# Attention and two gated layers in one kernel: the order in which the next pair's q and k are prepared, the padding of the last keys' v, and the place of three weight conversions

## The chip, the cores and the metric

The kernel runs on one core of a Trainium2 chip. The metric is the device time of one execution in microseconds (us), as the median of the runs shown. Profile numbers come from one further execution that was recorded instruction by instruction.

## The reference

The reference is a thresholded attention followed by two gated layers. There are 4 batches of 8 heads, 576 positions and 64 dimensions a head; q, k and v are float32, the weights float64.

```
scores = scale * q @ k.T                       # per head, 576 x 576
thresh = max(scores, -1) - tau
scores = where(scores >= thresh, scores, -1e9)
attn   = exp(scores - max) / (sum + 1e-9)
x = (attn @ v) as 2304 tokens x 512
g = x @ w_gate;  x = (silu(g) * (x @ w_val)) @ w_out         # 512 -> 1536 -> 512
h = (x @ w1) * (x @ w2) @ w3;  out = h @ w_out2              # 512 -> 1024 -> 512
```

## The kernel before

Each float32 operand of a matmul is split into a high part of TensorE's short float type and the low remainder, and products are summed from both parts. Splitting is therefore everywhere: a high part is a rounding copy, a low part a subtraction.

**Attention** goes over 16 pairs of heads (p, four pairs to a batch). One pair has nine tiles (i = 0 to 8): four row blocks of 128 for each head, and tile 4, which holds the last 64 rows of both. For each tile `mm_scores` makes scores in one of two S banks of PSUM, `el_max` (L482, VectorE) takes the negative row maximum and moves the scores to P, `el_exp` (L491, ScalarE) makes the exponential, and `el_mask` (L501, VectorE) applies the threshold. Scores are issued two tiles ahead, masks two tiles behind, so that the scores of the next pair's first tile are issued in tile 7 of this one.

The **main queue** holds the work behind the masks: transposes of P through TensorE (`it_T`, `it_kl`, `it_lq`, `it_corner`), each split on its way out of PSUM on one of three paths (`evac_split`), and the products with v (`it_pv`). Five items of a pair are queued behind its tile 4's mask, eleven behind tile 8's, which is two tiles into the next pair. The **prep queue** holds the preparation of the next pair. `it_k` and `it_q` transpose k and q through TensorE and copy the high part out on ScalarE (khi, qhi); `it_k2` and `it_q2` subtract it in PSUM by a matmul (`less`), copy out the low part (klo, qlo), and stack high and low parts into the operands L and R by twelve DMAs on SyncE's queue (`stack`, L348 and L349). `it_left` transposes the last 64 rows of q and k (L421) and writes LZ and part of R (L313). Every transpose, split and product with v takes one of four T banks of PSUM. `some` gives both queues credit: 19.5 main items for nine tiles, 0.8 prep items a tile. What is appended to `deferred` by one item runs after the next one (`run_item`). The compiler orders each engine's instructions by a simulated time with the program's order as priority; so instructions can move ahead of their place in the program where buffers allow it.

**The last keys' v.** 64 rows of v behind the first 512 are split for a whole batch by `split_left` into vls; `split_v` copies each pair's share by two DMAs into VLZ, which holds zeros in the other head's half of the partitions.

**Weights** come as float64 and are turned into float32 in place of two halves. `conv_step` loads raw words (three buffers, 512 KB each, L128), takes them apart on VectorE (L139, L142, L145) and ScalarE (L148, L149) and joins them on GpSimd (L150); one step later `conv_value` finishes (L157) and `conv_unit` splits the value into a slot of two parts (L196, L199, the latter in turn on GpSimd and VectorE). The **slots** are shared by weights and token blocks: 3 from the start (u1), 7 more at the last pair's start (u2), 8 more near its end (u3), 24 after attention (u4). In the last pair `early` interleaves three conversion steps with the preparation of x block 0 (`x_prep`, four pieces; each takes two raw slots for its loads, L790 and L795, adds on GpSimd at L826, multiplies on VectorE at L829 and splits at L817 and L818). The gated layer's matmuls (L835) on x block 0 need all four pieces and the first three weight units.

Of the kernel before, what the change touches and what calls it, by code (L numbers as in the profile page):

```python
# [23 lines left out]
N_U1, N_U2, N_U3, N_U4 = 3, 7, 8, 24  # L24
N_TMP, N_BIG, N_HB, N_TA = 6, 3, 3, 1

GROUP = 2

# [6 lines left out]
def kernel(  # L35
# [171 lines left out]

    def conv_step(n=1):

        old = []  # L210
        while conv_mid and conv_mid[0][2]() and len(old) < n:
            old.append(conv_mid.popleft())
            old[-1][1](conv_value(old[-1][0]))
# [14 lines left out]
    def attention(actx, early, tail):  # L228
# [8 lines left out]
        ta = lctx.enter_context(tc.tile_pool(name="ta", bufs=N_TA))  # L237
        raw_i, in_tail = [0], []

        def raw_tile():  # L240
            raw_i[0] += 1
            if in_tail or raw_i[0] % (N_TA + N_TMP) >= N_TA:
                return tmp()
            return ta.tile([P, 512], F32, tag="raw", name="raw")

# [7 lines left out]
        VLZ = at.tile([P, 2, 2, 2, D], F32R, name="VLZ")  # L253
        nc.gpsimd.memset(f32(VLZ), 0.0)

# [29 lines left out]
        def split_left(b):  # L285
# [11 lines left out]
            vls = wk.tile([P, HP, 2, D], F32R, tag="vls", name="vls", bufs=2)  # L297
            split_pool(vls[:, :, 0, :], vls[:, :, 1, :], vl)
            lsplit[b] = (qks, vls)

        def split_v(p):
# [4 lines left out]
            vls = lsplit[p // HP][1]  # L306
            for h in range(2):
                r = slice(64 * h, 64 * h + 64)
                nc.sync.dma_start(out=f32(VLZ[r, p % 2, h]), in_=f32(vls[r, p % HP]))
            load(p + 2, (2,))  # L310

# [39 lines left out]
        halves = {}  # L351

        def it_q(p):
            hi = sp.tile([P, 512], F32R, tag="qhi", name="qhi")
            halves[p, 0] = (turn(raws.pop((p, 0)), hi, 0.125), hi)

        def it_k(p):
            hi = sp.tile([P, 512], F32R, tag="khi", name="khi")
# [774 lines left out]
```

## Time and profile before

| | |
|---|---|
| median of 3 runs | 1189.6 us (1189.56 to 1189.74) |
| profiled execution | 1189.26 us |
| its span, first to last instruction | 1187.3 us |
| TensorE matmul busy | 1122.1 us, 95% |
| TensorE weight load busy | 959.8 us, 81% |
| VectorE busy | 733.1 us, 62% |
| ScalarE busy | 590.3 us, 50% |
| GpSimd busy | 475.7 us, 40% |
| mean granted TensorE clock | 0.991 of full speed |

PE is TensorE, PEld its weight loads (they overlap the matmuls), DVE VectorE, ACT ScalarE, POOL GpSimd, SP SyncE. Busy time is the union of an engine's instructions in a stretch. A matmul's end is modelled, so that a PE that is busy throughout need not be at its peak rate. L12 is line 12 of the kernel; where a helper issues an instruction, the line is the helper's. "t_bank<-ident,P" names what an instruction writes and reads.

### The profile page before, as it was taken

The page shows a single profiled execution, that of the slowest core. Times are in us where ns is not written, and L with a number is a line of the kernel's source. Part 1 is how long each engine was busy: PE and PEld are TensorE (multiplying, and loading weights), DVE is VectorE, ACT ScalarE, POOL GpSimd, SP SyncE. Part 2 cuts the span into 40 slices and gives each one's busy share as a digit, 9 for nine tenths or more (in the row PEclk, how much of TensorE's full clock was granted, in tenths as well). Part 3 has the DMA queues.
Part 4 walks back from the last instruction along what each step waited for, and adds up shares of the span by engine and source line. Part 5 has one row for each costly group of instructions (what it writes and reads, how often), then busy time and mean ns, then how long its engine had stood idle before and what let it go on. Part 6 is the DMA issues. An engine that isn't in the chain of part 4 may idle for free.

```text
span 1187.3 us, 16882 instructions
## 1 busy us (share of the span) xinstructions
PE 1122.1 (95%) x6074; PEld 959.8 (81%) x6074; DVE 733.1 (62%) x1272; ACT 590.3 (50%) x1071; POOL 475.7 (40%) x457
## 2 busy tenths in 40 slices
PE   7898998899878999999999999999899999999998
PEld 6788888788766777888888888888787888888886
DVE  7987868778798797656464664567892022432222
ACT  6877878778786456443242432345563231321111
POOL 4575665565663655443232332234241221321110
PEclk9999999999989999999999999999999999999999
DMA  8865756656455743222111120123430010100024
GB/s 197 224 146 141 163 132 142 146 121 142 107 170 167 216 126 100 75 68 71 31 59 36 37 89 8 47 93 103 124 107 18 1 36 1 37 1 1 1 58 102
DMA packets 107891, 108.14 MB, mean 91 GB/s; under 512 B 48800, under 2 KB 82208, under 8 KB 107808
## 3 DMA queue, kind: packets, MB, share of 16 engines
q1 hardware_dynamic: 107808, 107.06, 34.3%
q8 instruction: 48, 0.79, 0.3%
q14 instruction: 35, 0.29, 0.1%
HBM read 68.16 MB, written 14.23 MB: 69 GB/s over the span
## 4 chain that ended last, share of the span: by engine, by line
PE 55%; DVE 5%; DMA 2%; ACT 1%; issue 1%; POOL 0%; POOLq 0%; DVEq 0%; ACTq 0%
PE t_bank L835 36%; PE s_bank L835 19%; DMA raw<-in_moe_w_dram 2%; DVE tmp L157 1%; DVE slot L818 1%; DVE raw L142 1%; DVE tmp L145 1%; DVE tmp L139 0%; DVE slot L911 0%; PE t_bank L908 0%; DVE slot L199 0%; DVE slot L1022 0%; DVE slot L882 0%; DVE slot L1059 0%; ACT raw L148 0%
## 5 line engine op out<-in xcount | busy, mean ns | idle before, releaser
L835 PE MATMUL t_bank<-slot,slot 128*128 128x512 f32 (+1 forms) x2592 | 559.7, 371 | 5.9 <-DVE slot L818 2.4
L835 PEld LDWEIGHTS t_bank<-slot,slot 128*128 128x128 f32 x2592 | 457.0, 189 | 92.8 <-DVE slot L818 3.3
L835 PE MATMUL s_bank<-h,slot 128*128 128x512 f32 (+1 forms) x720 | 161.9, 372 | 3.4 <-ACT slot L884 2.2
L150 POOL TENSOR_TENSOR raw<-raw 128x512 int32<-128x512 int32 x76 | 84.4, 1111 | 182.1 <-ACT raw L149 171.6
L501 DVE SCALAR_TENSOR_TENSOR P<-P,stat,E 128x576 f32<-128x576 f32 x144 | 148.3, 1043 | 5.6 <-POOL stat L474 3.9
L835 PEld LDWEIGHTS s_bank<-h,slot 128*128 128x128 f32 x720 | 126.8, 190 | 27.1 <-ACT slot L884 2.6
L482 DVE TENSOR_SCALAR_CACHE_REDUCE P<-s_bank,neg 128x576 f32<-128x576 f32 x144 | 114.2, 809 | 55.2 <-PE s_bank L443 55.2
L1069 DVE TENSOR_TENSOR tmp<-tmp,t_bank 128x512 f32<-128x512 f32 (+1 forms) x40 | 25.3, 633 | 178.2 <-PE t_bank L835 178.2
L107 POOL TENSOR_TENSOR h<-tmp,h 128x512 fp32r<-128x512 f32 (+1 forms) x60 | 74.4, 1239 | 136.1 <-ACT h L106 136.0
L1073 POOL TENSOR_TENSOR h<-tmp,h 128x512 fp32r<-128x512 f32 (+1 forms) x38 | 45.8, 1205 | 200.5 <-ACT h L1071 200.5
L491 ACT ACTIVATE E<-P,stat 128x576 f32<-128x576 f32 x144 | 116.4, 812 | 9.7 <-DVE P L482 8.8
L443 PE MATMUL s_bank<-R,L 128*128 128x288 f32 x512 | 101.2, 318 | 14.7 <-DVE P L482 5.6
L920 DVE TENSOR_TENSOR tmp<-tmp,t_bank 128x512 f32<-128x512 f32 (+1 forms) x60 | 37.9, 631 | 113.1 <-PE t_bank L835 104.5
L835 PE MATMUL s_bank<-slot,h 128*128 128x512 f32 x432 | 106.6, 391 | 0.9 <-DVE slot L1059 0.8
L328 PE MATMUL t_bank<-ident,P 128*128 128x128 f32 x640 | 90.5, 277 | 14.5 <-DVE AT L524 4.7
L443 PEld LDWEIGHTS s_bank<-R,L 128*128 128x128 f32 x512 | 76.8, 194 | 26.7 <-DVE P L482 15.1
L835 PEld LDWEIGHTS s_bank<-slot,h 128*128 128x128 f32 x432 | 79.9, 188 | 18.3 <-DVE slot L1059 2.1
L882 DVE TENSOR_TENSOR slot<-s_bank,slot 128x1024 f32<-128x1024 f32 (+1 forms) x72 | 82.2, 1146 | 18.5 <-PE s_bank L835 16.5
L328 PEld LDWEIGHTS t_bank<-ident,P 128*128 128x128 f32 x640 | 74.2, 141 | 23.5 <-DVE ATL L524 4.6
L583 PE MATMUL t_bank<-AT,sp 128*128 128x288 f32 x512 | 87.5, 307 | 5.3 <-DVE AT L524 2.4
L157 DVE SCALAR_TENSOR_TENSOR tmp<-tmp,raw 128x512 f32<-128x512 f32 x76 | 72.0, 948 | 30.5 <-POOL raw L150 30.5
L919 ACT ACTIVATE tmp<-t_bank 128x512 f32<-128x512 f32 (+1 forms) x60 | 33.2, 554 | 113.3 <-PE t_bank L835 106.9
(110 smaller groups left out, 1427.9 us busy)
## 6 DMA issues: line engine op xcount, KB each, us to landing
raw<-in_moe_w_dram SPq DMA_DIRECT2D x32, 512.0 KB, 3.8
raw<-in_moe_w_out_dram SPq DMA_DIRECT2D x20, 512.0 KB, 3.5
x_dram<-xs SPq DMA_DIRECT2D x64, 144.0 KB, 2.4
L<-qhi SPq DMA_DIRECT2D x60, 128.0 KB, 2.9
L<-qlo SPq DMA_DIRECT2D x60, 128.0 KB, 2.5
raw<-in_moe_w_gate_dram SPq DMA_DIRECT2D x12, 512.0 KB, 3.7
raw<-in_moe_w_val_dram SPq DMA_DIRECT2D x12, 512.0 KB, 3.8
ld<-in_k_dram SPq DMA_DIRECT2D x16, 256.0 KB, 4.0
```

What stands on the lines that cost most here:

```text
L107: nc.gpsimd.tensor_tensor(out=lo, in0=src, in1=f32(hi), op=ALU.subtract)
L150: nc.gpsimd.tensor_tensor(out=a, in0=a, in1=x, op=ALU.subtract)
L157: nc.vector.scalar_tensor_tensor(out=f32(m), in0=f32(m), scalar=2.0 ** 20, in1=f32(a), op0=ALU.add, op1=ALU.mult)
L328: nc.tensor.matmul(bank[:, t * P:(t + 1) * P], lhsT=part, rhs=ident, is_transpose=True, start=(t == 0), stop=(t == len(parts) - 1),)
L443: nc.tensor.matmul(o, lhsT=lhs, rhs=R[:, c:c + HALF], start=(h == hs2[0] and e == 0), stop=(h == hs2[-1] and e == 1),)
L482: nc.vector.tensor_scalar(out=p_tile(p, i).rearrange("p (a c) -> p a c", a=2), in0=sb[:, :, 0:HALF], scalar1=neg, scalar2=None, op0=ALU.mu ...
L491: nc.scalar.activation(out=e, in_=p_tile(p, i), func=ACTF.Exp, scale=-1.0, bias=stats[p // HP][:, 0, c:c + 1],)
L501: nc.vector.scalar_tensor_tensor(out=t, in0=t, scalar=stats[b][:, 1, c:c + 1], in1=e, op0=ALU.is_le, op1=ALU.mult, accum_out=sums[b][:, c: ...
L583: nc.tensor.matmul(o, lhsT=vs[:, 4 * h + c, :, :].rearrange("p a d -> p (a d)"), rhs=AT[h][:, e, c, cs], start=(c == 0 and e == 0), stop=F ...
L835: nc.tensor.matmul(o, lhsT=lhs(a), rhs=rhs(c), start=(first and i == 0), stop=(last and i == 2))
L882: nc.vector.tensor_tensor(out=a, in0=s, in1=a, op=ALU.add)
L1073: (nc.vector if end else nc.gpsimd).tensor_tensor(out=h[:, 1, 0:n], in0=ab[:, 0:n], in1=f32(h[:, 0, 0:n]), op=ALU.subtract)
```

## The change

Three things change. First, `turn` takes both halves of the split: it transposes, copies the high part out, and appends the second half with its stacking DMAs to `deferred`; `it_k2` and `it_q2` are gone as items, and the prep queue is given 1.0 items a tile. Second, `split_left` writes the last keys' v straight into zero-padded tiles, one for each of two batches, by four GpSimd instructions on 64 partitions each; vls and the two DMAs a pair are gone. Third, in tile 4 of pairs 3, 6 and 9 a conversion step and its finishing half (`conv_end`) are added to the prep queue, so that the first three weight units fill the slots of u1 there; `early` keeps x block 0 alone, the raw loads at half of attention are gone, u2 has one slot less and u3 one more, and the extra buffer for raw evacuations (`ta`) is gone.

```diff
-N_U1, N_U2, N_U3, N_U4 = 3, 7, 8, 24
-N_TMP, N_BIG, N_HB, N_TA = 6, 3, 3, 1
+N_U1, N_U2, N_U3, N_U4 = 3, 6, 9, 24
+N_TMP, N_BIG, N_HB = 6, 3, 3
+EARLY = (3, 6, 9)
...
+    def conv_end(n=1):
+        old = 0
+        while conv_mid and conv_mid[0][2]() and old < n:
+            bits, done, _ = conv_mid.popleft()
+            done(conv_value(bits))
+            old += 1
+        return old
...
     def conv_step(n=1):
-        old = []
-        while conv_mid and conv_mid[0][2]() and len(old) < n:
-            old.append(conv_mid.popleft())
-            old[-1][1](conv_value(old[-1][0]))
+        old = conv_end(n)
...
-        VLZ = at.tile([P, 2, 2, 2, D], F32R, name="VLZ")
-        nc.gpsimd.memset(f32(VLZ), 0.0)
+        VLZ = [at.tile([P, HP, 2, 2, D], F32R, name=f"VLZ{n}") for n in range(2)]
+        for t in VLZ:
+            nc.gpsimd.memset(f32(t), 0.0)
...
-            vls = wk.tile([P, HP, 2, D], F32R, tag="vls", name="vls", bufs=2)
-            split_pool(vls[:, :, 0, :], vls[:, :, 1, :], vl)
-            lsplit[b] = (qks, vls)
+            for h in range(2):
+                r = slice(64 * h, 64 * h + 64)
+                split_pool(VLZ[b % 2][r, :, h, 0, :], VLZ[b % 2][r, :, h, 1, :], vl[r])
+            lsplit[b] = qks
...
-            vls = lsplit[p // HP][1]
-            for h in range(2):
-                r = slice(64 * h, 64 * h + 64)
-                nc.sync.dma_start(out=f32(VLZ[r, p % 2, h]), in_=f32(vls[r, p % HP]))
...
-        def turn(raw, hi, scale):
+        def turn(raw, hi, lo, scale, then):
             bank = t_bank()
             turn_p(bank, [raw[:, t, :, :].rearrange("p h d -> p (h d)") for t in range(4)])
             nc.scalar.activation(out=hi, in_=bank, func=ACTF.Copy, scale=scale)
-            return bank
-        def turn_lo(bank, hi, lo, scale):
-            less(bank, minus_r if scale == 1.0 else minus8_r, hi)
-            nc.scalar.activation(out=lo, in_=bank, func=ACTF.Copy, scale=scale)
+            def rest():
+                less(bank, minus_r if scale == 1.0 else minus8_r, hi)
+                nc.scalar.activation(out=lo, in_=bank, func=ACTF.Copy, scale=scale)
+                then()
+            deferred.append(rest)
...
-                raw = raw_tile()
+                raw = tmp()
...
-            return [lambda f=f: f(p) for f in (it_k, it_q, it_k2, it_q2, it_left)]
+            return [lambda f=f: f(p) for f in (it_k, it_q, it_left)]
...
-            credit[1] += (1.5 if in_tail else 0.8) * frac
+            credit[1] += (1.5 if in_tail else 1.0) * frac
...
-            if n == NS // 2:
-                conv_fetch()
+            if i == 4 and p in EARLY:
+                prep.extend([conv_step, conv_end])
...
-        r = [conv_step] * 3
-        for kk in range(KD):
-            r.insert(2 * kk + 1, lambda kk=kk: x_prep(0, kk))
-        return r
+        conv_fetch()
+        return x_items(0)
```

## Rows read from the trace of the kernel before

**Rows 1.** The page, part 1: busy us, share of the span, instructions.

```profile
PE 1122.1 (95%) x6074; PEld 959.8 (81%) x6074; DVE 733.1 (62%) x1272; ACT 590.3 (50%) x1071; POOL 475.7 (40%) x457
```

**Rows 2.** Stretches: bounds, us, busy us of each engine, PEclk, DMA share, GB/s.

```profile
core 0: us, PE busy (x) PEld busy (x) DVE busy (x) ACT busy (x) POOL busy (x), PEclk, DMA share, GB/s
176.78:191.17 14.39, 11.88 (x87) 10.60 (x85) 13.58 (x34) 13.78 (x27) 9.90 (x11) 1.00 0.70 163
191.17:198.06 6.89, 6.89 (x55) 6.82 (x56) 2.64 (x7) 3.70 (x12) 1.69 (x2) 1.00 0.44 101
...
47.62:329.77 282.15, 254.29 (x1827) 231.79 (x1828) 226.72 (x517) 228.85 (x463) 169.36 (x191) 0.99 0.61 142
329.77:361.00 31.23, 22.90 (x136) 19.51 (x135) 31.23 (x58) 25.36 (x47) 18.94 (x16) 0.89 0.58 170
...
456.00:814.00 358.00, 358.00 (x1752) 303.45 (x1753) 205.59 (x279) 135.59 (x218) 123.03 (x104) 1.00 0.19 60
```

**Rows 3.** Waits, 16 to 330 us: who waited for whom, us, times, longest.

```profile
DVE P L482 <- PE s_bank L443: 50.6, 16, 6.3
```

**Rows 4.** Timeline of ACT in pair 8: start us, us, line, operation.

```profile
179.54 0.62 ACT L340 ACTIVATE khi<-t_bank 128x512 fp32r<-128x512 f32 x1
...
182.41 0.66 ACT L345 ACTIVATE klo<-t_bank 128x512 fp32r<-128x512 f32 x1
...
184.26 0.60 ACT L340 ACTIVATE qhi<-t_bank 128x512 fp32r<-128x512 f32 x1 [0.45 <-PE t_bank L328]
...
186.65 0.61 ACT L345 ACTIVATE qlo<-t_bank 128x512 fp32r<-128x512 f32 x1
...
194.99 0.39 ACT L313 ACTIVATE R<-t_bank 128x128 fp32r<-128x128 f32 x2
```

**Rows 5.** Timeline of SyncE's queue in pair 8.

```profile
180.19 0.49 SPq L348 DMA_DIRECT2D R<-khi  x1
...
184.25 0.66 SPq L282 DMA_DIRECT2D ld<-in_q_dram  x1
...
190.83 0.60 SPq L349 DMA_DIRECT2D L<-qhi  x1
```

**Rows 6.** Timeline of PE at the end of pair 8.

```profile
186.02 0.70 PE L443 MATMUL s_bank<-R,L 128*128 128x288 f32 x4
...
191.12 0.51 PE L443 MATMUL s_bank<-R,L 128*128 128x288 f32 x2 [0.85 <-DVE P L501]
...
194.22 0.46 PE L421 MATMUL t_bank<-ident_r,qkls 128*128 128x128 f32 x4
```

**Rows 7.** Timeline of DVE at the end of pair 8.

```profile
196.88 0.82 DVE L482 TENSOR_SCALAR_CACHE_REDUCE P<-s_bank,neg 128x576 f32<-128x576 f32 x1 [4.25 <-PE s_bank L443]
```

**Rows 8.** Groups on DVE, 330.5 to 358.4 us: count | busy us, mean ns | idle.

```profile
L157 DVE SCALAR_TENSOR_TENSOR tmp<-tmp,raw 128x512 f32<-128x512 f32 x3 | 4.2, 1411 | 0.0
...
L145 DVE SCALAR_TENSOR_TENSOR tmp<-raw,tmp 128x512 f32<-128x512 uint16 x3 | 2.4, 816 | 0.0
L142 DVE TENSOR_SCALAR raw<-raw 128x512 int32<-128x512 int32 x3 | 2.4, 812 | 0.0
...
L199 DVE TENSOR_TENSOR slot<-tmp,slot 128x512 fp32r<-128x512 f32 x1 | 1.7, 1749 | 0.0
L139 DVE TENSOR_SCALAR tmp<-raw 128x512 int32<-128x512 int32 x3 | 1.2, 455 | 0.0
```

**Rows 9.** Groups on ACT in the same stretch.

```profile
L148 ACT ACTIVATE raw<-raw,ebias 128x512 int32<-128x512 int32 x3 | 2.3, 758 | 1.0 <-DVE tmp L145 1.0
```

**Rows 10.** Timeline of SyncE's queue in pair 1.

```profile
38.61 0.60 SPq L128 DMA_DIRECT2D raw<-in_moe_w_gate_dram  x1
```

**Rows 11.** Timelines of the last pair: SyncE's queue, and all engines.

```profile
326.43 0.55 SPq L790 DMA_DIRECT2D slot<-x_dram  x1
...
360.66 0.68 DVE L818 TENSOR_TENSOR slot<-tmp,slot 128x512 fp32r<-128x512 f32 x1
```

**Rows 12.** VLZ's instructions (min/median/max ns), and groups of the first 650 us.

```profile
L309 SPq DMA_DIRECT2D VLZ<-vls x32: 461/476/1601, 10.2 to 329.6; - x32
...
L103 POOL TENSOR_TENSOR vls<-vl,vls 128x256 fp32r<-128x256 f32 x4 | 3.6, 894 | 0.2
```

More of the change, by code (lines that the diff above doesn't have):

```diff
@@ L236, in attention @@
         sp = lctx.enter_context(tc.tile_pool(name="sp", bufs=1))
[L237 to L244, printed above, removed]
+        in_tail = []
         ATT = at.tile([P, 2, 2, 4, S], F32R, name="AT")
@@ L305, in split_v @@
             splits[p, 2] = t
-            vls = lsplit[p // HP][1]
-            for h in range(2):
-                r = slice(64 * h, 64 * h + 64)
-                nc.sync.dma_start(out=f32(VLZ[r, p % 2, h]), in_=f32(vls[r, p % HP]))
             load(p + 2, (2,))
+        deferred = deque()
         def scaled(out_, in_, scale=1.0):
@@ L349, in stack, with then @@
             nc.sync.dma_start(out=f32(dst[64:P, :]), in_=f32(bottom[64 * h:64 * h + 64, :]))
-        halves = {}
         def it_q(p):
+            L, R = qk_tiles(p)
             hi = sp.tile([P, 512], F32R, tag="qhi", name="qhi")
-            halves[p, 0] = (turn(raws.pop((p, 0)), hi, 0.125), hi)
+            lo = sp.tile([P, 512], F32R, tag="qlo", name="qlo")
+            def then():
+                stack(L[:, 0, :], lo, hi, 0)
+                stack(L[:, 1, :], hi, lo, 1)
+                stack(L[:, 2, :], hi, lo, 0)
+                stack(L[:, 3, :], lo, hi, 1)
+            turn(raws.pop((p, 0)), hi, lo, 0.125, then)
         def it_k(p):
+            L, R = qk_tiles(p)
             hi = sp.tile([P, 512], F32R, tag="khi", name="khi")
-            halves[p, 1] = (turn(raws.pop((p, 1)), hi, 1.0), hi)
-        def it_q2(p):
-            L, R = qk_tiles(p)
-            bank, hi = halves.pop((p, 0))
-            lo = sp.tile([P, 512], F32R, tag="qlo", name="qlo")
-            turn_lo(bank, hi, lo, 0.125)
-            stack(L[:, 0, :], lo, hi, 0)
-            stack(L[:, 1, :], hi, lo, 1)
-            stack(L[:, 2, :], hi, lo, 0)
-            stack(L[:, 3, :], lo, hi, 1)
-        def it_k2(p):
-            L, R = qk_tiles(p)
-            bank, hi = halves.pop((p, 1))
             lo = sp.tile([P, 512], F32R, tag="klo", name="klo")
-            turn_lo(bank, hi, lo, 1.0)
-            stack(R[:, 0:512], hi, lo, 0)
-            stack(R[:, 640:1152], lo, hi, 1)
+            def then():
+                stack(R[:, 0:512], hi, lo, 0)
+                stack(R[:, 640:1152], lo, hi, 1)
+            turn(raws.pop((p, 1)), hi, lo, 1.0, then)
         def turn_r(parts, dst):
@@ L412, in it_left @@
             L, R = qk_tiles(p)
-            qks = lsplit[b][0]
+            qks = lsplit[b]
             bank = t_bank()
@@ L504, in el_mask @@
             )
-        deferred = deque()
         path_i = [0]
@@ L588, in it_pv @@
                 nc.tensor.matmul(
-                    o, lhsT=VLZ[:, p % 2, h, :, :].rearrange("p a d -> p (a d)"),
+                    o, lhsT=VLZ[b % 2][:, hp, h, :, :].rearrange("p a d -> p (a d)"),
                     rhs=ATL[:, e, cs], start=False, stop=(e == 1),
```

## The prediction

> **What bounds the kernel now.** The page comes first. TensorE (PE) is busy 95% of the span [rows 1], so I looked for the stretches where it is not. The view of stretches gives three regimes. From 456 to 814 us PE is busy 358.0 of 358.0 us: nothing that moves work on another engine helps there, and whatever is saved earlier shifts this block forward whole. From 329.8 to 361.0, the last pair of heads (pair 15), VectorE (DVE) is busy 31.23 of 31.23 us and PE 22.90. In the thirteen steady pairs 2 to 14, from 47.62 to 329.77 us, no engine is full: PE 254.3, DVE 226.7, ScalarE (ACT) 228.9 of 282.15 us [rows 2]. That is 21.7 us a pair, with 17.6 us of ACT work in it.
>
> Cutting one steady pair in two shows why. Pair 8 begins with its first exponential at 176.78 and runs its nine tiles until 191.17; ACT is busy 13.78 of these 14.39 us and DVE 13.58. Then come 6.89 us until pair 9's first exponential, in which PE is busy throughout, but ACT only 3.70 us and DVE 2.64 [rows 2]. The two halves hardly overlap. In the table of waits for 16 to 330 us, DVE's row-maximum instruction waits 50.6 us for score matmuls, in only 16 waits of 3.2 us each, about one for each pair boundary [rows 3].
>
> What those scores wait for is seen by following the preparation of pair 9 through pair 8, times from pair 8's start. The first half of k leaves ACT at +2.8 us (khi), its second at +5.6 (klo), the first half of q at +7.5 (qhi), its second at +9.9 (qlo) [rows 4]. Twelve stacking DMAs follow on SyncE's queue, one each 0.6 us when it isn't waiting; the first goes at +3.4, the last is issued at +14.1 [rows 5]. Pair 8's last scores run at 186.02; the first two matmuls of pair 9 start 4.4 us behind them, at 191.12 (+14.3), with the last stacks. The left-over rows' transposes (`it_left`) come at 194.22 (+17.4) [rows 6], write R at 194.99 [rows 4], and the first maximum of pair 9, which needs that column of R, starts at 196.88 [rows 7]. The other boundaries have the same order: stacks, first scores, `it_left`, maximum. So the period is set by a chain of preparation whose last two links, q's second half and `it_left`, are late because they stand late in the program.
>
> **The change, part by part.**
>
> *Order of the preparation.* Before, five items at 0.8 a tile: credit reaches 1, 2, 3, 4, 5 in tiles 1, 2, 3, 4 to 5 and 6, so `it_left` is emitted in tile 6, behind nearly all of the previous pair's transposes and P·V items, whose PSUM banks it then follows. After, three items at 1.0 a tile: `it_k` in tile 0, `it_q` in tile 1, `it_left` in tile 2; k's second half runs behind `it_q`, q's behind the next main item. No instruction of k, q or the left-over rows is added or removed. `it_q` and `it_left` now stand ahead of the P·V items. With khi still at about +2.8, q's transposes come one item behind k's, qlo some 3 us earlier, and the stacks run nearly back to back: 12 of 0.6 us plus the two loads of the pair after next (0.7 us each) from +3.4 end near +12 rather than +14.1. `it_left` is done by about +8. Then the first scores may start near +12, the maximum 1.5 us later and the exponential 1.2 us after that (196.88 to 198.06 here): a chain of about 15 us instead of 21.7. It no longer decides; what is late next is engine work: ACT's 17.6 us a pair, and PE's 19.6 busy. So a pair may fall to anything between 17.6 and 21.7 us. Four in-order queues with all this work interleaved will not fill any of them: I take 20.6, a little over a quarter of the way down. 13 pairs x 1.1 us = **-14.3 us**. Bounds: 0 and -36 (18.9 us a pair, ACT at 93%).
>
> *Three units of weights in pairs 3, 6 and 9.* Each costs, in the last pair's rows, DVE 4.0 us (L139, L142, L145, L157 and every second time L199: 1.2 + 2.4 + 2.4 + 4.2 + 1.7 = 11.9 for three) [rows 8], and ACT two conversions of 0.76 us (L148, and L149 like it) [rows 9] and a cast of 128x512, 0.62 as khi's [rows 4], 2.1 us in all; GpSimd takes the rest. They now fall into tiles 5 and 6 of a pair, where ACT and DVE are nearly full. ACT is 81% busy over the pairs, so I charge 0.81 x 2.1 = 1.7 us each, **+5.1 us**. Bounds: 0 (in the idle part) and 4.0 each, 12. The first three raw loads were already issued at 38.6 us although the program has them at pair 8 [rows 10]; the compiler's order pulls loads ahead, so I cost their move at nothing. Three more raw loads of 512 KB move to pairs 3, 6 and 9 behind the freeing of a raw buffer; they stand on SyncE's queue in front of P·V outputs, not of stacks, which are done by tile 5: nothing, or 1 us each if they hold up a stack.
>
> *The last pair.* The 11.9 us of DVE work above leave a stretch in which DVE is full for 31.23 us [rows 2, 8]. Cover is not the question, but what is late next: the first GLU step needs all four pieces of x block 0. Their first load goes at 326.43, and the last one's low half is written by 361.34 [rows 11]: 8.7 us a piece, with DVE full. After, 6 free slots stand where 10 stood; four become x block 0, so one pair of raw slots serves the four pieces in turn: load, GpSimd add, DVE multiply, next load. The trace has no such chain; with DVE free I estimate 7.5 us a piece, 30 in all (bounds: 4 us, if loads and arithmetic overlap, and 11), and it may start earlier, since the stacks and `it_left` of pair 15, whose buffers lie in its place, end earlier. Saved: at most 11.9, I take **-8 us**; at worst 0. Behind 361 the count of conversions ahead of the GLU steps is the same from the second step on, so the gain should be carried through to the block from 456.
>
> *Last keys' v.* 32 small DMAs go (0.48 us of issue each, two a pair) [rows 12] from a queue that has gaps; the trace shows no P·V matmul that waits for them. GpSimd gets four instructions a batch instead of two, on half the partitions but as long in each: at most 2 x 0.89 = 1.8 us more a batch [rows 12]; GpSimd is 60% busy in the pairs [rows 2]. **0**, bounds -2 and +4. The two bigger cleared tiles lie before GpSimd's first use of them: 0. Dropping the extra raw tile leaves six buffers for three such evacuations a pair: 0.
>
> The Trainium skill's page "SBUF — State Buffer", section "SBUF: two separate sides", states that a GpSimd instruction and a DVE one with two SBUF inputs lock each other out for the whole instruction. It speaks against both the v split and the units beside the pairs. The rows agree in kind: L157, with two such inputs, took 1411 ns on average in the last pair, the DVE form of L199 1749 [rows 8]. By that rule the v split costs DVE up to 1.8 us a batch, 7 us in all, and the sum below would be 7 us higher.
>
> **Sum.** -14.3 + 5.1 - 8 = -17.2 us. The profiled execution took 1189.3 us (span 1187.3 and 2 us around it): 1172.1; the median of the runs is 0.3 above it: **1172.4 us**.
>
> **The rivals.**
> (a) *The pairs keep their length.* The chain shortens, but the T banks of PSUM (four, through which every transpose, split and P·V passes) or ACT set the pace, and the wait at the boundary turns into one for a bank. For it: k's bank is held from its transposes to klo, at least from khi's start to klo's end, 3.5 us [rows 4], and deferring need not shorten that; ACT is full in the tile stretch. Against: ACT and DVE stand half idle for 6.9 us of each pair. Then +5.1 - 8: 1186.7 (1183 to 1190).
> (b) *x block 0 is as late as before.* One pair of raw slots makes its four loads serial; from 8.7 us a piece on it ends no sooner than before and the last pair's 8 us are lost: 1180.4 (1177 to 1185).
> (c) *Slower.* The pairs are held by DVE's in-order queue, so that each unit costs its whole 4.0 us there, the pairs gain nothing, and only the 8 us come back: 1189.6 + 12 - 8 = 1193.6 (1190 to 1199). It decides from 2.7 us a unit on if the pairs stay as long.
> (d) *The two halves overlap fully:* 18.9 us a pair: -36 + 5 - 8, 1150 (1145 to 1160).
>
> **How the numbers follow.** Forecast (1162 to 1180) 0.47; (a) 0.17; (b) 0.13; (c) 0.13; (d) 0.10. About 0.2% of the time, 2.4 us, is what a measurement can tell from no change. Faster by more: forecast, (b), (d) and 0.07 of (a), 0.77; within: 0.10 of (a); slower: (c), 0.13. The range 1157 to 1191 takes in the forecast, (a), (b) and the edges of (c) and (d).
>
> **What would show it.** Right: `it_left` by +8 and the last stack by +12 of each pair; the 50.6 us of DVE's wait for scores under 25; pairs near 20.6; no conversion in pair 15 before x block 0 and the pair well under 31 us; the GLU block begins about 17 us earlier and stays as long. Wrong: pairs still 21 us and more with PE waiting for ACT or a T bank; pairs 3, 6, 9 longer than their neighbours by 4; x block 0 finished no nearer to pair 15's start than the 31.6 us of now (361.34 less 329.77).

## The result

The changed kernel takes 1196.5 us (median of 6 runs, 1193.5 to 1202.5) against 1189.6 us before (6 runs); the ratio is 1.0071 (95% interval 1.0047 to 1.0096). It is slower, 24 us above the forecast and outside its range of 1157 to 1191 us. The profiled execution took 1193.5 us, its span 1191.7.

Milestones of the two profiled executions, in us from the span's start:

| | before | after |
|---|---|---|
| first exponential of pair 2 | 47.6 | 45.7 |
| first exponential of pair 15 | 329.8 | 335.4 |
| length of a pair, 2 to 14, by first exponentials | 21.70 | 22.28 |
| last product with v of pair 13 ends | 327.6 | 340.8 |
| end of the last exponential | 361.0 | 354.6 |
| x block 0 split | 361.3 | 367.3 |
| end | 1187.3 | 1191.7 |

By their first exponentials pairs 2 to 14 lose 7.5 us together, where 14.3 less 5.1 were to be gained. This mark flatters the changed kernel, since there the first exponential of a pair runs ahead of products with v that stood in front of it before: 1786 matmuls lie between the two marks instead of 1827. By the last product with v of pair 13 the changed kernel is 13.2 us late. Pair 15 is 12 us shorter, as its conversions have gone. x block 0, for which the gated layer waits, ends 31.9 us behind pair 15's first exponential, as late as before (31.6), but 26.5 us behind pair 13's last product instead of 33.7.

The view of stretches of the changed kernel answers to [rows 2]; pair 8 is cut at the end of its last exponential.

```profile
core 0: us, PE busy (x) PEld busy (x) DVE busy (x) ACT busy (x) POOL busy (x), PEclk, DMA share, GB/s
175.53:191.37 15.84, 14.28 (x106) 12.84 (x104) 12.80 (x32) 13.26 (x27) 8.53 (x11) 1.00 0.62 148
191.37:200.42 9.05, 8.21 (x41) 7.59 (x40) 3.82 (x10) 4.54 (x12) 2.18 (x2) 0.62 0.32 70
45.71:335.40 289.69, 252.40 (x1786) 229.26 (x1786) 233.93 (x530) 232.44 (x469) 167.43 (x197) 0.97 0.60 137
335.40:354.58 19.18, 16.28 (x119) 14.76 (x118) 16.23 (x38) 15.51 (x31) 11.30 (x12) 1.00 0.49 136
460.00:818.00 358.00, 357.83 (x1758) 303.18 (x1757) 205.99 (x278) 136.91 (x220) 124.99 (x105) 1.00 0.19 59
```

The boundary between the two halves of a pair has not closed. It was 6.89 us with PE busy throughout; it is 9.05 us, PE idles in it, and its clock is granted at 0.62. The block behind 460 us is as full as before, so that what is lost ahead of it goes straight to the end. Now the waits that answer to [rows 3], from 16 to 335 us (who waited for whom, us, times, longest):

```profile
DVE P L480 <- PE s_bank L441: 25.9, 28, 3.1
...
PE s_bank L441 <- DMA L<-qlo: 8.2, 10, 1.5
PEld s_bank L441 <- DMA L<-qlo: 2.9, 5, 1.5
PEld s_bank L441 <- DMA L<-qhi: 1.9, 2, 1.1
```

DVE's wait for scores has halved, nearly as foretold (50.6 to 25.9 us, under 25 in the forecast), and nothing was gained by it. TensorE itself now waits for the stacks, 8.2 us by its own row. The rows of PEld lie at the same boundaries and partly in the same time; one or the other waits for 10.4 us in all. In the kernel before it is 2.6 us, with these rows:

```profile
PE s_bank L443 <- DMA L<-qlo: 2.1, 4, 1.3
PEld s_bank L443 <- DMA L<-qlo: 1.1, 2, 0.6
```

What that looks like is seen on PE's timeline of the changed kernel at the end of pair 8, beside [rows 6] (L441 scores, L580 and L585 the products with v, L327 turns, L419 the left-over rows; in brackets the idle time ahead and what ended it):

```profile
187.22 0.68 PE L441 MATMUL s_bank<-R,L 128*128 128x288 f32 x4
...
188.35 0.65 PE L327 MATMUL t_bank<-ident,P 128*128 128x128 f32 x4 [0.23 <-ACT klo L344]
189.50 0.54 PE L419 MATMUL t_bank<-ident_r,qkls 128*128 128x128 f32 x4 [0.50 <-ACT qlo L344]
190.73 0.63 PE L327 MATMUL t_bank<-ident,P 128*128 128x128 f32 x4 [0.70 <-DVE ATL L521]
...
193.47 0.82 PE L441 MATMUL s_bank<-R,L 128*128 128x288 f32 x2 [0.84 <-DMA L<-qlo]
194.09 1.91 PE L327 MATMUL t_bank<-ident,P 128*128 128x128 f32 x8
195.65 2.27 PE L580 MATMUL t_bank<-AT,sp 128*128 128x288 f32 x8
197.72 0.67 PE L585 MATMUL t_bank<-ATL,VLZ 128*128 128x288 f32 x2
198.20 0.99 PE L441 MATMUL s_bank<-R,L 128*128 128x288 f32 x6
```

The left-over rows do come ahead of pair 9's first scores now (189.50; before 194.22, behind them). But the first scores, which wait for the last stacks, also stand ahead of all four products with v of pair 7. Before, the first product ran at 188.45, ahead of the scores at 191.12, and filled the time in which the stacks landed:

```profile
188.45 1.32 PE L583 MATMUL t_bank<-AT,sp 128*128 128x288 f32 x8 [0.18 <-ACT AT L518]
...
191.12 0.51 PE L443 MATMUL s_bank<-R,L 128*128 128x288 f32 x2 [0.85 <-DVE P L501]
```

### The profile page after: what moved, and what is told of

It is laid out like the page before. It is cut to its first block, busy times and chain, and to the rows that moved or that the text cites. A ratio compares the mean times of both kernels' runs of the same rounds, so it can differ in the third digit from the quotient of the medians.

```text
span 1191.7 us, 16832 instructions
## 1 busy us (share of the span) xinstructions
PE 1123.8 (94%) x6074; PEld 961.7 (81%) x6074; DVE 721.0 (61%) x1272; ACT 590.0 (50%) x1071; POOL 472.7 (40%) x466
## 4 chain that ended last, share of the span: by engine, by line
PE 65%; DVE 15%; DMA 7%; POOL 5%; issue 4%; ACT 4%; SPq 1%; ACTq 0%; DVEq 0%; POOLq 0%
PE t_bank L832 36%; PE s_bank L832 19%; DVE P L499 4%; PE t_bank L580 4%; DVE P L480 3%; PE s_bank L441 2%; PE t_bank L327 2%; DMA L<-qlo 2%; DMA raw<-in_moe_w_dram 2%; DVE slot L815 1%; ACT E L489 1%; DVE tmp L159 1%; DVE tmp L147 1%; PE t_bank L585 1%; DVE tmp L826 1%
## 5 line engine op out<-in xcount | busy, mean ns | idle before, releaser
L499 DVE SCALAR_TENSOR_TENSOR P<-P,stat,E 128x576 f32<-128x576 f32 x144 | 145.3, 1025 | 18.4 <-POOL stat L472 10.7
L489 ACT ACTIVATE E<-P,stat 128x576 f32<-128x576 f32 x144 | 114.3, 800 | 20.8 <-DVE P L480 20.6
L441 PE MATMUL s_bank<-R,L 128*128 128x288 f32 x512 | 100.1, 317 | 20.5 <-DMA L<-qlo 8.2
L327 PE MATMUL t_bank<-ident,P 128*128 128x128 f32 x640 | 94.0, 282 | 13.0 <-DVE AT L521 2.9
L441 PEld LDWEIGHTS s_bank<-R,L 128*128 128x128 f32 x512 | 76.5, 194 | 34.7 <-DVE P L480 18.4
L159 DVE SCALAR_TENSOR_TENSOR tmp<-tmp,raw 128x512 f32<-128x512 f32 x76 | 69.1, 909 | 39.2 <-POOL raw L152 39.2
L327 PEld LDWEIGHTS t_bank<-ident,P 128*128 128x128 f32 x640 | 75.4, 144 | 21.5 <-ACT klo L344 4.5
L150 ACT ACTIVATE raw<-raw,ebias 128x512 int32<-128x512 int32 x76 | 58.0, 764 | 66.4 <-DVE tmp L147 52.6
L580 PE MATMUL t_bank<-AT,sp 128*128 128x288 f32 x512 | 84.5, 302 | 3.4 <-DVE AT L521 3.4
```

The lines of the kernel that those rows point to most:

```text
L150: nc.scalar.activation(out=a, in_=x, func=ACTF.Relu, scale=8.0, bias=ebias[:, 0:1])
L159: nc.vector.scalar_tensor_tensor(out=f32(m), in0=f32(m), scalar=2.0 ** 20, in1=f32(a), op0=ALU.add, op1=ALU.mult)
L327: nc.tensor.matmul(bank[:, t * P:(t + 1) * P], lhsT=part, rhs=ident, is_transpose=True, start=(t == 0), stop=(t == len(parts) - 1),)
L441: nc.tensor.matmul(o, lhsT=lhs, rhs=R[:, c:c + HALF], start=(h == hs2[0] and e == 0), stop=(h == hs2[-1] and e == 1),)
L489: nc.scalar.activation(out=e, in_=p_tile(p, i), func=ACTF.Exp, scale=-1.0, bias=stats[p // HP][:, 0, c:c + 1],)
L499: nc.vector.scalar_tensor_tensor(out=t, in0=t, scalar=stats[b][:, 1, c:c + 1], in1=e, op0=ALU.is_le, op1=ALU.mult, accum_out=sums[b][:, c: ...
```

## The experiments

**First question: which part costs?** The change is exactly three parts: A the order of preparation, B the padding by GpSimd, C the early units. The first theories were that k's and q's T banks, held together until their second halves, starve the other turns (Theory 1, later B), and that the early units cost more than charged (Theory 2).

e1_prep is the kernel before with part A alone, e2_vlz with part B alone, e3_early with part C alone, e4_noprep with B and C.

```diff
...
-            return [lambda f=f: f(p) for f in (it_k, it_q, it_k2, it_q2, it_left)]
+            return [lambda f=f: f(p) for f in (it_k, it_q, it_left)]
...
-            credit[1] += (1.5 if in_tail else 0.8) * frac
+            credit[1] += (1.5 if in_tail else 1.0) * frac
```

> The kernel before with the new preparation alone: both halves of the split in one item with the second half deferred, three items at 1.0 a tile. Theory 1 (T banks): k and q now hold two of the four T banks together for some 5.4 us, in the stretch in which the previous pair's transposes need them, so pairs 2 to 14 grow from 21.7 us to about 22.2 and the kernel takes 5 to 8 us more than before. Theory 2 (the early weight units are what costs): the preparation changes nothing, 1189 +- 2. My prediction's own step said 14 us less, 1175.

1207.1 us, ratio 1.0153 (1.0131 to 1.0176). The order of preparation alone costs 18 us, more than Theory 1 expected. Its waits, 46 to 346 us, show the same row as the changed kernel's, larger; with the rows for qhi and those of PEld, which lie partly in the same time, one or the other waits for 18.6 us:

```profile
PE s_bank L444 <- DMA L<-qlo: 12.6, 10, 3.1
```

```diff
-            vls = wk.tile([P, HP, 2, D], F32R, tag="vls", name="vls", bufs=2)
-            split_pool(vls[:, :, 0, :], vls[:, :, 1, :], vl)
+            for h in range(2):
+                r = slice(64 * h, 64 * h + 64)
+                split_pool(VLZ[b % 2][r, :, h, 0, :], VLZ[b % 2][r, :, h, 1, :], vl[r])
...
```

> The kernel before with the last keys' v written to padded tiles by GpSimd alone, with what it brings for memory: no extra raw tile, one slot fewer in u2 and one more in u3. All theories: within 2 us of before. If it is 4 us or more slower, GpSimd's instructions or the missing slot cost, which neither theory has.

1188.5 us, ratio 0.9998 (0.9987 to 1.0009): nothing.

```diff
+            if i == 4 and p in EARLY:
+                prep.extend([conv_step, conv_end])
...
```

> The kernel before with the three weight units beside pairs 3, 6 and 9 alone; seven slots in u2 as before. Theory 1: pairs 3, 6 and 9 grow by 1 to 2 us each, pair 15 falls from 31 us to about 20, x block 0 is finished about as long after pair 15's start as before, so the whole is within 3 us of before. Theory 2: 5 to 8 us slower, from pairs 3, 6 and 9.

1185.0 us, ratio 0.9969 (0.9958 to 0.9980): the units gain. Pair 15 starts 2.6 us later and x block 0 is done at 356.3 instead of 361.3 us.

> The changed kernel with the old preparation put back (five items at 0.8 a tile, the halves apart), padding by GpSimd and early units kept. Theory 1: pairs return to about 21.7 us and the kernel to 1187 to 1192, 5 to 8 us less than the changed one. Theory 2: it stays at 1194 to 1198.

1183.1 us, ratio 0.9947 (0.9929 to 0.9964). So the whole loss is part A, and Theory 2 falls. The end of pair 13's last product says the same: 330.4 us in e4, 10.4 ahead of the changed kernel, and the two spans end 10.3 us apart.

The wait at the stacks is not this loss by itself, as e4's row for it is nearly the changed kernel's (first line, 16 to 335 us). In pairs 2 to 14 PE idles for 28.2 us in e4 (second line, 285.08 less 256.86), 27.9 before and 37.3 in the changed kernel. Of the 9 us more than in e4, 8 stand ahead of work in T banks, where PE idles for 19.5 us instead of 11.6.

```profile
PE s_bank L440 <- DMA L<-qlo: 8.1, 8, 2.7
```

```profile
47.51:332.59 285.08, 256.86 (x1827) 233.49 (x1828) 232.82 (x530) 234.18 (x473) 173.82 (x199) 0.98 0.61 141
```

**Second question: what in the order of preparation?** Deferring (Theory D), the T banks (Theory B), or the earlier place of the items, of the left-over rows above all (Theory L). e5_pace is e4 with its five old items, only at earlier places.

```diff
-            credit[1] += (1.5 if in_tail else 0.8) * frac
+            credit[1] += (1.5 if in_tail else 1.25) * frac
```

> The kernel with padding and early units and the old preparation (1183 us), but its five items at 1.25 a tile, so that k and q are turned in tiles 0 and 1, their second halves and the left-over rows follow by tile 3. Theory B (k's and q's T banks are held at the same time, ahead of the previous pair's transposes) and theory L (the left-over rows' early place) expect 1190 to 1198. Theory D (it is the deferring behind the next item) expects 1181 to 1186.

1199.7 us, ratio 1.0084 (1.0050 to 1.0117): slow without any deferring. e6_defer_near and e7_defer_apart do the opposite, deferring at the old places (`nop` is an empty item).

```diff
-            return [lambda f=f: f(p) for f in (it_k, it_q, it_left)]
+            return [lambda f=f: f(p) for f in (it_k, it_q, nop, nop, it_left)]
...
-            credit[1] += (1.5 if in_tail else 1.0) * frac
+            credit[1] += (1.5 if in_tail else 0.8) * frac
```

> The changed kernel with its deferred halves, but at the old pace of 0.8 and with two empty items, so that k is turned in tile 1, q in tile 2 and the left-over rows in tile 6, as before the change. Theory B: k and q still hold banks together, 1190 to 1198. Theory D: the same. Theory L: 1181 to 1186.

1181.6 us, ratio 0.9940 (0.9920 to 0.9959): the deferring is innocent, and k and q side by side, with both banks held, are fast too, which speaks against Theory B. e7 has the items k, nop, q, nop, left at 0.8:

> As the run before, but with an empty item between k and q, so that q is turned in tile 3 to 4, when k's bank is free again. Theory B: 1181 to 1186. Theory D: 1190 to 1198. Theory L: 1181 to 1186.

1185.1 us, ratio 0.9968 (0.9946 to 0.9989). Setting the banks apart gains nothing over e6. e8_nobank takes the banks out directly, in the changed kernel: the low parts of q and k are made from the high parts in SBUF and the subtracting matmul is left out, so that a bank is free behind the first copy.

```diff
-                less(bank, minus_r if scale == 1.0 else minus8_r, hi)
-                nc.scalar.activation(out=lo, in_=bank, func=ACTF.Copy, scale=scale)
+                nc.scalar.activation(out=lo, in_=f32(hi), func=ACTF.Copy, scale=scale)
```

> The changed kernel, but the low parts of q and k are a copy of the high parts in SBUF: the subtracting matmul is left out, ScalarE's instruction and the stacking DMAs stay. A T bank is then free after the high part, some 3.5 us earlier, 7 us of 64 us of bank time a pair. Theory B: pairs fall from 22.3 us to 20.5 or less, 1165 to 1178. Theories D and L: 1190 to 1197, but for 0.2 us of PE a pair.

1190.8 us, ratio 1.0012 (0.9994 to 1.0030): of the 1.24 points between the changed kernel (1.0071) and e4 (0.9947), 0.59 come back, with two matmuls a pair less. The banks are half of it at most, and PE's idle time ahead of work in T banks hardly falls (18.6 us). e9_left_late and e10_left_early split the place of the items: in e9 the left-over rows alone are late (k, q, three times nop, left, at 1.0), in e10 k and q alone (k, q, left at 0.8).

> The changed kernel with two places per item left empty between q and the left-over rows: k and q stay as early as in the changed kernel, the left-over rows come about three tiles later (about where the kernel before has them). Theory L (the left-over rows' early place, which holds a T bank and writes LZ and R in the middle of the pair, is what costs): time falls to that of the delayed variants, 1180 to 1186 us. Rival Q (k and q one tile earlier is what costs; the left-over rows are innocent): 1192 to 1198 us, as the changed kernel. Anything between says that both share it.

> The changed kernel with the rate of preparation items at 0.8 a tile and nothing between: k and q are as late as in the fast variant (1181.6 us), the left-over rows come right behind them, tiles earlier than there. Theory L (left-over rows' place): 1190 to 1198 us. Rival Q (k's and q's place): 1180 to 1186 us.

1190.3 us, ratio 1.0012 (0.9998 to 1.0026), and 1189.0 us, ratio 0.9999 (0.9987 to 1.0011). Either place gives back about half (0.59 and 0.72 points); neither Theory L nor Rival Q has it alone. Neither place alone is the cause then; the next question is what both of them move.

**Third question: is it the wait for the stacks?** e11_free_before and e12_free_after keep all work and cut the scores of pairs 2 to 15 off from their own stacks; they read pair 1's.

```diff
         def qk_tiles(p):
+            if p >= 2:
+                return lrs[0]
...
-            L, R = lrs[p]
+            L, R = lrs[min(p, 1)]
```

> The kernel before, with the scores of pairs 2 to 15 read from pair 1's stacks, and the preparation writing its stacks, copies and left-over rows as before into pair 0's tiles that nobody reads any more: all its instructions and transfers stay, but no scores wait for them (the left-over rows' LZ still does). What is computed is not the reference's from pair 2 on. Theory P (the prediction's: the period of a pair is set by the preparation, at its end by the landing of the stacks): pairs 2 to 14 fall from 21.7 to 20.6 us or less, 1175 us or less. Theory M (the period is set by the main chain: turns of P, copies out of the T banks, products with v, at 21.7 us; the wait for the stacks at the pair's start is slack that is filled again): pairs stay at 21.4 to 21.8 us, 1184 to 1191 us.

> The changed kernel with the same cut: scores of pairs 2 to 15 from pair 1's stacks, all preparation done but read by nobody. Theory W (in the changed kernel TensorE waits in order for the stacks at the start of the scores with nothing else to run, and its clock drops behind that): pairs fall from 22.3 to 21.4 to 21.8 us, half-clock time from 17 to under 10 us, 1179 to 1186 us. Rival V (the place of the items on the T banks costs by itself, whether or not the scores wait): pairs stay at 22.1 us or more, 1190 us or more.

1177.9 us, ratio 0.9896 (0.9879 to 0.9913), and 1177.0 us, ratio 0.9898 (0.9886 to 0.9911). By first exponentials pairs 2 to 14 take 20.1 and 20.9 us instead of 21.7 and 22.3. Two stretches, the first from e11, the second from e12:

```profile
48.13:309.20 261.07, 243.33 (x1771) 223.27 (x1772) 222.49 (x516) 223.12 (x453) 151.38 (x186) 0.99 0.64 148
```

```profile
46.51:317.68 271.17, 246.73 (x1783) 225.16 (x1783) 234.73 (x531) 230.85 (x467) 163.95 (x196) 0.99 0.64 145
```

Rival V falls, and so does Theory M, by which the main chain sets the period whatever the stacks do. Theory W's signs are met, by more than it said. Theory P's time of 1175 is missed, and its price, 1.6 us a pair by first exponentials, needs care: fewer matmuls lie between the marks here too (1771 against 1827), and the end moves by only 11.3 us (1187.3 to 1176.0) where the marks move by 21.1. By the last product with v of each pair (the column "by v" below) the cut is worth 1.0 us a pair in the kernel before and 1.3 in the changed one.

The two kernels come out at the same time, but not by the same pairs. e12's are longer than e11's by 0.6 us by v, and its last pair is shorter. If the order cost nothing without the wait, e12 should lie below e11 by what padding and early units bring, 0.53 points in e4; it lies 0.02 above. So, as an estimate, some 0.55 of the 1.24 points that the order costs stay when no scores wait (about 0.3 either way, from the three intervals). A kernel with the old order, both other parts and the cut would settle it and was not run. What does go with the cut is the idle time ahead of work in T banks: 11.8 us in e12, as in e4.

**The loop.** A pair is thus a closed chain: first scores of pair p, then products with v and turns of P, then the turn of k for pair p+1, then its twelve transfers, then the first scores of p+1. Its legs, worked out from the trace of each run's profiled execution as means over p = 3 to 13: S-k from the first scores to the start of khi, k-st from there to the issue of the last stack, st-S from there to the next first scores. Two counts come from the order of TensorE's instructions as compiled, means over the same pairs: PV is how many of the 32 main matmuls of the products with v of pair p-2 stand ahead of pair p's first scores; Sc is how many of the 40 score matmuls of pair p stand ahead of k's turn for p+1. Half is the time at half clock in pairs 2 to 14. "Pair" is the length of pairs 2 to 14 by first exponentials, "by v" that of pairs 1 to 13 by the end of the last product with v. All in us but the counts. The profiled executions of e7, e10 and e19 were the slowest of their runs (1192.5, 1193.7 and 1181.6 us), that of the changed kernel the fastest.

```
run              median  pair  by v   S-k  k-st  st-S    PV    Sc   half
before           1189.6  21.7  21.9  10.3  10.2   1.0  10.3  13.8    6.8
after            1196.5  22.3  22.8  14.5   8.7   0.1   0.0  25.8   17.1
e1_prep          1207.1  23.1  23.7  14.8   8.6   0.8   0.0  26.2   30.7
e4_noprep        1183.1  21.9  22.2  10.2  10.4   1.1  11.0  13.8   10.2
e5_pace          1199.7  22.7  23.0  14.6   8.4   0.2   0.0  26.9   17.1
e6_defer_near    1181.6  21.7  21.9  10.2  10.2   1.0  11.0  13.8    6.8
e7_defer_apart   1185.1  21.8  22.1   6.6  12.9   2.5  25.9  10.5   13.7
e8_nobank        1190.8  22.0  22.5  14.3   8.3   0.2   0.0  26.5   22.3
e9_left_late     1190.3  22.5  22.5  13.2   8.6   0.8   0.0  13.8   13.7
e10_left_early   1189.0  22.3  22.8  10.4  10.2   2.0   9.5  21.1   16.9
e11_free_before  1177.9  20.1  20.9  19.0  10.0  -8.6   0.0  31.3    3.4
e12_free_after   1177.0  20.9  21.5  18.7   8.7  -6.3   0.0  29.8    6.8
e14_stack_act    1256.2  26.5  26.5  17.1   7.3   2.4   0.0  28.7   85.3
e15_near_act     1206.0  23.3  23.3  12.2   8.4   2.9   3.9  13.8   34.1
e16_near_main    1179.5  21.4  21.5   9.0  10.9   1.8  15.3  12.0    6.8
e17_before_act   1175.4  20.8  20.6   9.0   9.0   2.6  15.7  13.5    0.0
e18_best         1173.6  20.9  20.9   9.0   9.3   2.6  15.5  13.8    3.4
e19_best_main    1177.6  21.3  21.5   8.5  10.5   2.4  16.1  11.6   10.2
```

The new order does what it was for: from khi to the last stack it is 8.7 us instead of 10.2. But the leg ahead of it grows from 10.3 to 14.5 us, in each run with the early places (after, e1, e5, e8). With the preparation early, the compiled order has the first scores of a pair ahead of every product with v of two pairs before, and k's turn behind these and behind 26 of the pair's own 40 score matmuls. So when PE sits at the first scores until the stacks have landed, the products with v, the turns of P and the next k are all queued behind it, and the delay goes round the loop. The order and the legs are read from the traces; that this queueing is what makes the leg longer is argued from them. For it: freeing the banks leaves the leg at 14.3 us (e8), and the idle time ahead of work in T banks goes when the scores don't wait (e12). In e9 and e10 the two counts part, and each keeps about half of the loss by its ratio. In e11 and e12 the order is at its worst (PV 0, Sc about 30) and the pairs are short, since the scores don't wait. So the wait carries part of what the order costs, by the estimate above about half; why the rest stays is open.

**Fourth question: does shortening a leg help?** Six of the twelve transfers are issued by ScalarE instead of SyncE in e14 (changed kernel), e15 (e6) and e17 (kernel before).

```diff
         def stack(dst, top, bottom, h):
...
-            nc.sync.dma_start(out=f32(dst[64:P, :]), in_=f32(bottom[64 * h:64 * h + 64, :]))
+            nc.scalar.dma_start(out=f32(dst[64:P, :]), in_=f32(bottom[64 * h:64 * h + 64, :]))
```

> The kernel before with the six transfers issued by ScalarE and nothing else. Loop theory: the leg from k's turn to the stacks (12.0 us) shortens by 1 to 2 us and the pairs with it, from 21.7 to 20.6 to 21.2 us, 1178 to 1185 us. Rival (period set by the main chain or by ScalarE): 1188 us or more.

1175.4 us, ratio 0.9896 (0.9878 to 0.9915), better than expected. Two legs fall, k-st by 1.2 and S-k by 1.3 us, and st-S grows by 1.6; PE has no half clock in the pairs. The edit changed the compiled order too: 15.7 of the 32 products with v stand ahead of the scores instead of 10.3. What the issues and what this order bring was not separated. Its timeline at the same place as above:

```profile
185.69 1.30 PE L583 MATMUL t_bank<-AT,sp 128*128 128x288 f32 x8
...
187.09 1.23 PE L583 MATMUL t_bank<-AT,sp 128*128 128x288 f32 x8
...
189.58 0.43 PE L443 MATMUL s_bank<-R,L 128*128 128x288 f32 x2
189.84 0.46 PE L421 MATMUL t_bank<-ident_r,qkls 128*128 128x128 f32 x4
190.35 0.50 PE L443 MATMUL s_bank<-R,L 128*128 128x288 f32 x2
```

> The changed kernel with the lower half of each stack (six of the twelve transfers a pair) issued by ScalarE instead of SyncE, where twelve issues in a row take 7.7 us (185.3 to 193.0 in pair 8). Loop theory: the stacks land 2 us or more earlier behind k's turn (9.8 us on the mean of pairs 3 to 13), the pairs fall from 22.3 to 21.5 us or less, 1182 to 1189 us, although TensorE's order stays that of the changed kernel. Rival V (the items' place costs by itself): pairs stay at 22 us or more, 1192 us or more. Rival A: the issues cost ScalarE what they save, no change against 1196.

> The fast variant (changed kernel, both preparations at 0.8 a tile next to each other, the left-over rows late; 1181.6 us) with the same six transfers issued by ScalarE. Loop theory: the leg from k's turn to the stacks (11.4 us) shortens by 2 us, pairs towards 20.6 to 21.2 us, 1172 to 1180 us. Rival: 1181 to 1185 us, as ScalarE pays for the issues or TensorE's order turns to that of the changed kernel.

1256.2 us, ratio 1.0568 (1.0544 to 1.0591), and 1206.0 us, ratio 1.0146 (1.0125 to 1.0166): against what the loop theory expected, and far beyond Rival A. In e14 the leg k-st does fall (8.7 to 7.3 us), and S-k grows by more. ScalarE's timeline of e14 shows where: its own issues (ACTq) stop the copies queued behind them, here from 168.6 to 173.3 us (in brackets its own idle time).

```profile
167.99 0.60 ACT L344 ACTIVATE qlo<-t_bank 128x512 fp32r<-128x512 f32 x1 [0.39 <-DMA ld<-in_k_dram]
171.02 0.47 ACTq L351 DMA_DIRECT2D L<-qhi  x1
172.18 1.12 ACTq L351 DMA_DIRECT2D L<-qlo  x2
173.33 0.21 ACT L563 CAST ATL<-t_bank 128x64 fp32r<-128x64 f32 x1 [4.74 <-DMA L<-qhi]
```

In the table of its waits from 46 to 390 us this row is ScalarE's largest, where e17 has none like it:

```profile
ACT ATL L563 <- DMA L<-qhi: 22.5, 8, 4.7
```

What exactly the issue at 171.02 waits for was not isolated. In e15 ScalarE's waits at such transfers are smaller (10.9 us in all, 46 to 355 us, against 29.5 in e14). There the leg k-st falls from e6's 10.2 to 8.4 us, as the loop theory expected, but the compiled order turned towards that of the changed kernel, as the rival had it: PV 3.9 instead of 11.0, S-k 12.2 us instead of 10.2. The loop theory's forecasts fail in both; as neither run moved the one leg alone, they decide neither for the loop nor against it. e16_near_main moves the other leg, in e6, by a faster main queue:

```diff
-            credit[0] += 19.5 / 9 * frac
+            credit[0] += 27 / 9 * frac
```

> The fast variant with the main queue at 27 items for nine tiles instead of 19.5, so that the products with v of the pair before come earlier against the scores (8 to 23 of their 32 first matmuls now stand ahead of the next pair's first scores in the compiled order, 0 to 21 in the fast variant). Loop theory: the leg from the first scores to k's turn (10.6 us) shortens, pairs 21.0 to 21.6 us, 1175 to 1181 us. Rival (the order of the products with v against the scores doesn't matter): 1181 to 1183 us.

1179.5 us, ratio 0.9926 (0.9908 to 0.9943), 2 us under e6, though the intervals overlap: S-k falls by 1.2 us, while k-st grows by 0.7 and st-S by 0.8.

**Both together.** e18_best is e4 with e17's line; e19_best_main adds e16's.

> The old order of preparation with the padding by GpSimd, the early units, and six of the twelve stack transfers a pair issued by ScalarE. If the parts add: 1175.4 us less the 4.8 us that padding and units saved without ScalarE's issues (1183.1 against 1187.9 to 1188.6), 1168 to 1172 us. If the early units now cost their full ScalarE and VectorE time, as the pairs at 20.8 us have no wait left to hide them: 1173 to 1177 us.

> The same with the main queue at 27 items for nine tiles. Loop theory with slack left: 1 to 3 us under the one before, as it was 2.1 us there without ScalarE's issues. If the pairs have come to another bound (TensorE's own work, about 20 us a pair with nothing waited for): no difference within 1.5 us.

1173.6 us, ratio 0.9858 (0.9833 to 0.9882), and 1177.6 us, ratio 0.9893 (0.9875 to 0.9910). e18 beats both kernels. Its time lies in the range of the costly units, 1173 to 1177; its ratio, taken against the kernel before on the same chip, is 0.38 points under e17's, where the two parts alone brought 0.53 (e4), so that they add for the most part, and the two readings can't be told apart here. e19 is 4.0 us slower than e18, which neither of its expectations had: S-k falls by 0.5 and k-st grows by 1.2 us.

## Why the prediction was wrong

**Order of the preparation, forecast -14.3 us: this is the step that failed.** In the whole change it costs 13.4 us (1196.5 less e4's 1183.1; by the ratios 1.24 points, 14.7 us). Its reading of the kernel before holds: the boundary wait is a wait for preparation, and taken away outright it gives 12.4 us by e11's ratio, 1.0 us a pair by v (1.1 was charged). What failed is the sentence "with khi still at about +2.8". Pair 8 in the changed kernel, from its first exponential at 175.53 (ScalarE, then SyncE's queue, beside [rows 4, 5]):

```profile
183.98 0.62 ACT L340 ACTIVATE khi<-t_bank 128x512 fp32r<-128x512 f32 x1
...
185.59 0.58 ACT L340 ACTIVATE qhi<-t_bank 128x512 fp32r<-128x512 f32 x1
...
187.68 0.62 ACT L344 ACTIVATE klo<-t_bank 128x512 fp32r<-128x512 f32 x1
...
188.83 0.61 ACT L344 ACTIVATE qlo<-t_bank 128x512 fp32r<-128x512 f32 x1
```

```profile
185.28 0.65 SPq L350 DMA_DIRECT2D R<-khi  x1
...
192.39 0.60 SPq L351 DMA_DIRECT2D L<-qhi  x1
```

khi stands at +8.5; over pairs 3 to 13 its mean is +9.4 (+3.2 before). From there the chain runs as foretold: qlo 4.9 us behind khi (before 7.1), the last stack 8.4 us behind it (before 11.3). The prediction measured the chain from the pair's start and took its beginning as fixed; it closed the chain at the first maximum and did not follow it back from the first scores to k's turn. It also counted it as a gain that `it_left` comes ahead of the products with v, and did not ask what else then stands ahead of them in PE's order: the first scores, with their wait. That this wait, in front of the products with v and the turn of k, makes khi late is shown in part only, as said under e12. By its own signs, `it_left` came at +14.0 (+8 foretold), the last stack at +16.9 (+12), the pairs at 22.3 us (20.6).

**Early units, forecast +5.1 us:** e3 puts pair 15's start 2.6 us later (332.3 against 329.8 us, e4 332.6), and pair 13's last product 2.5 (e4 2.8). Half of the charge; the sign was right.

**Last pair, forecast -8 us:** right in size. In e4 x block 0 is done 23.7 us behind pair 15's start instead of 31.6, which is -7.9 us. In the changed kernel it is 31.9 by that mark, which looks like rival (b), though a single pair of raw slots served e4 as well. But 49 matmuls more than in e4 run there between pair 15's start and the gated layer's first matmul, late products with v among them. From pair 13's last product on it is 26.5 us in the changed kernel, 25.9 in e4 and 33.7 before: the gain came, and what is lost was lost ahead of it. How the products hold x block 0 up is seen on SyncE's queue and on GpSimd in the changed kernel, and on GpSimd in e4:

```profile
333.08 0.54 SPq L787 DMA_DIRECT2D slot<-x_dram  x1
...
338.77 4.40 SPq L596 DMA_DIRECT2D x_dram<-xs  x4
344.64 0.36 SPq L787 DMA_DIRECT2D slot<-x_dram  x1
```

```profile
340.92 0.62 POOL L102 TENSOR_SCALAR sp<-ld 128x512 fp32r<-128x512 f32 x1 [2.92 <-PE t_bank L580]
...
343.32 1.29 POOL L823 TENSOR_TENSOR tmp<-slot 128x512 f32<-128x512 f32 x1
```

```profile
333.26 1.30 POOL L823 TENSOR_TENSOR tmp<-slot 128x512 f32<-128x512 f32 x1 [0.79 <-DMA slot<-x_dram]
```

The second load goes when the first piece's add (L823) has ended, at 344.61, and given its raw slots back. The add comes 10.2 us behind the first load, because GpSimd stands at the split of v, which waits for the late products; in e4 it comes 4.2 us behind. One reading was also wrong: 326.43 [rows 11] was not the first load of x block 0. One piece had been loaded at 48.6 us already; it was the second.

**Last keys' v, forecast 0:** right; e2 lies between 1.5 us faster and 1.1 slower. The Trainium skill's page "SBUF — State Buffer", section "SBUF: two separate sides", had been worked out to 7 us for this; e2 leaves no room for such a price here.

**The rivals.** The time is nearest to (c), 1193.6, whose mechanism e3 refutes. (a) named the T banks. Its sign did come, pairs over 21 us with PE idle ahead of work in T banks (19.5 us against e4's 11.6), but that idle time goes when the scores don't wait (e12), and e8 gives the banks half of the loss at most, with work removed as well. None named what the traces show: that an item's earlier place puts scores that wait in front of work that doesn't.

## What to carry to other kernels

Before a step is moved earlier to shorten a chain, follow that chain all the way round to its own beginning in the next turn of the loop, and ask of each in-order queue which waiting instruction would then stand ahead of which ready one. A wait that halves on one engine (here DVE's, 50.6 to 25.9 us) is no gain by itself: here idle time on the engine that feeds all others grew with it (27.9 to 37.3 us), while e17 has the first (27.4 us) without the second (19.8 us). To price a wait before building around it, run the kernel once with the dependence cut and the work kept, and read the price from the end of the kernel: here 12.4 us, while first exponentials, a mark that the cut itself moves, said 21. Then look for the cheapest way to shorten it: one line on who issues six transfers brought 12.6 us (1187.9 to 1175.4 on the same chip), nearly what the reordering had promised. The same line made the changed kernel 60 us slower and e6 24, so it has to be tried in the order in which it will run.

## What the runs showed of the hardware

The granted TensorE clock fell to half (1.2 of 2.4 GHz) in separate stretches. One of them, in the changed kernel's pair 8, with PE's idle times of 0.23, 0.50 and 0.70 us shortly before it (timeline above):

```profile
191.37:198.20 6.83, 5.99 (x26) 5.46 (x25) 2.25 (x6) 3.18 (x9) 2.18 (x2) 0.50 0.42 92
198.20:200.42 2.22, 2.22 (x17) 2.13 (x16) 1.57 (x4) 1.36 (x3) 0.00 (x0) 0.99 0.00 0
```

Eight matmuls of a product with v took 2.27 us in it, against 1.32 in the kernel before. Such time in pairs 2 to 14 goes from 0 us (e17) over 6.8 (before) and 17.1 (after) to 85.3 (e14), and the three slowest kernels have the most (e14, e15, e1). So PE's idle time may be paid for a second time in the clock; how much of what the pairs lose is the clock and how much the idle time was not separated.

Twelve stacking transfers issued by SyncE in a row took 7.7 us (185.3 to 193.0 us in the changed kernel's pair 8). An issue of one of them by ScalarE took 0.47 us in e14, but there ScalarE also stood for up to 4.7 us at such issues, with every copy and exponential behind it waiting too; in e17 its largest wait at these transfers was 0.2 us.
